# Branch A's output weights in three pieces, by 128, 104 and 24 partitions

## The chip, the core and the metric

The kernel runs on one core of one Trainium2 chip. The core has a matrix engine (TensorE, "PE" in the profile, its weight loads "PEld"), a vector engine (VectorE, "DVE"), a scalar engine (ScalarE, "ACT"), a general one (GpSimd, "POOL"), a sync engine that only issues transfers (SyncE, "SP"), 16 DMA engines that move data between the chip's memory (HBM) and the on-chip memory (SBUF, 128 partitions), and PSUM, where TensorE writes its sums. The metric is the device time of one execution in microseconds (us), lower is better. A time is compared with that of the kernel before, run on the same chip.

## What is computed

Two attention branches, A and B, each decode one token for two batch entries against a cache of 4096 tokens and 32 heads of 128 elements; a gate from the input mixes them:

```python
def _A_ref(x, k_cache, v_cache, wq, wo):          # x [2,1,512], caches [2,32,4096,128]
    q = (x @ wq).reshape(B, Sq, 32, 128).transpose(0, 2, 1, 3)
    scores = jnp.einsum("bhqd,bhkd->bhqk", q, k_cache) * (128 ** -0.5)
    p = _softmax(scores, axis=-1)
    o = jnp.einsum("bhqk,bhkd->bhqd", p, v_cache)
    return o.transpose(0, 2, 1, 3).reshape(B, Sq, 4096) @ wo   # wo [4096,512]
...
x = A_x
g = _sigmoid((x * gate_w).sum(-1, keepdims=True))
return g * a + (1 - g) * b                        # b: the same with B's caches and weights
```

Everything is float32. The caches are 4 x 134 MB, the four weight matrices 8.4 MB each: 570 MB have to be read once.

## The kernel before

**Tiles.** A unit is one batch entry and four heads of one branch: 16 units for A, 16 for B. A unit's K (and its V) is 16384 tokens of 128 elements, 128 rows of 64 KB, one row per partition. K goes into one of two 64 KB-per-partition tiles, `kt[0]` and `kt[1]`, in turn; V into the one tile `vt`. The weights use the K tiles too: the query weights `wq` of A and B come first, in `kt[0]` and `kt[1]`, and the output weights `wo` of A and B last, again in `kt[0]` and `kt[1]` (the table `place`, L206).

**Loops.** For each unit VectorE multiplies K by the query (L391) and sums over the 128 elements (L394), finds the maxima (L399 to L401) and makes the next query (L404, L405). ScalarE takes the exponentials (L365). TensorE multiplies these with V (L369), 32 chunks of four 32-row strips. A branch's 16 units run as loops on the engines, with semaphores between them that are written by hand.

**The order of the transfers.** All large loads are issued by SP, in one order written out in L516 to L526: `wq` A, first K, `wq` B, second K, first V, then K and V in turn; after the last K, `load_wo("A")`, the last V (in three pieces), and `load_wo("B")`. Before a K the wait is for its tile to be free (`k_free`, L231), before a V for `vt` (`v_free`, L239), before `wo` for the K tile (L245). The semaphore of a load counts 16 when all of it has landed.

**The output weights.** A matrix `wo` of 4096 by 512 lies as 32 rows of 512 elements (2 KB) in each of 128 partitions: partition p holds rows 32 p to 32 p + 31, which are 64 KB in one run in HBM. `load_wo` calls `load_parts`, which issues one load for each stretch of rows; for A a single stretch, 0 to OR = 32, on the semaphore slot "f"; for B six, with bounds 0, 16, 24, 28, 30, 31, 32 on six slots. `Streams.dma` (L97) issues a load and adds 16 to what the slot has to reach; it returns that semaphore and value, and `parts["wo", n]` keeps them.

**Who waits.** `arrived` (L213) makes an engine wait for pieces of a load. `project_out("A", OR)` (L575, body L489) waits once, before row 0, for entry 0 of `parts["wo", "A"]`; then it makes 32 products, one per row, into `most`. For B the products of rows 0 to 27 go into `most` too, with waits before rows 0, 16 and 24; ScalarE copies the sums out (L609), and the last rows (L512) and the fold of `most` (L612) are summed in another bank. Two copies (L621, L620) and two stores of the output end the kernel. Between A's product and that lie, on TensorE, branch B's `gather` (L473), the products with the last V (L369, `last_products`) and `deal_out("B")` (L482). POOL's L589 and what follows it reuse the tile of A's `wo`, and wait for A's product.

Of the kernel before, what the change touches and what calls it, by code (L numbers as in the profile page):

```python
# [12 lines left out]
P = 128  # L13
# [15 lines left out]
OR = H * DH // P  # L29
DQ = DH // OR  # L30
EARLY = OR - 4
# [110 lines left out]
def tile_gated_decode(ctx: ExitStack, tc: tile.TileContext, ins: dict, out: bass.AP):  # L142
# [12 lines left out]
    slot = small.tile([P, VC], F32, name="slot")  # L155
# [23 lines left out]
    with tc.tile_critical():  # L179
        S = Streams(nc, tc)  # L180
# [27 lines left out]
        parts = {}  # L208

        def load_parts(item, t, src, slots, *cuts):  # L210
            parts[item] = [S.dma("sp", t[:, i:j], src[:, i:j], slot=s) for s, i, j in zip(slots, cuts, cuts[1:])]
# [31 lines left out]
        def load_wo(n):  # L243
            i = place["wo", n]
            nc.sync.wait_ge(k_free[i], NU // 2)  # L245
            t = kt[i].rearrange("p r d -> p (r d)").rearrange("p (r e) -> p r e", e=D)
            for r in r_kt[i]:
                r.writers, r.readers = [], []
            load_parts(("wo", n), t, ins[n + "_wo"].rearrange("(p r) e -> p r e", p=P), *(
                ("f", 0, OR) if n == "A" else ("abchij", 0, OR // 2, 3 * OR // 4, EARLY, OR - 2, OR - 1, OR)))  # L250


        class Scratch:
# [8 lines left out]
        rows, ident, ones, xg, w, e = start(D), start(P), start(1), start(B * KC), start(P), start(1)  # L262
# [3 lines left out]
        def vput(e, make, reads=(), writes=(), **kw):  # L266
# [6 lines left out]
                                  slot="y"))  # L273
# [213 lines left out]
        wo = {}  # L487
# [33 lines left out]
        for u in range(2, NU):  # L521
            load_k(u)
            load_v(u - 1)
        load_wo("A")
        load_v(NU - 1)
        load_wo("B")  # L526

        spread_queries(0)
        for h in (0, 1):
            t = kt[0][:, h * NS // 2:(h + 1) * NS // 2]  # L530
            r = R()
# [84 lines left out]
        for i, e in enumerate(("dve", "act")):  # L616
            for j in range(STRIPS // OS):
                k = (i * STRIPS // OS + j) * QT
                src = acc[i][k:k + B, :D // STRIPS]
# [27 lines left out]
```

## Time and profile before

| | us |
|---|---|
| three runs, median | 1324.59 (1324.45 to 1324.62) |
| the profiled execution, its own time | 1324.58 |
| its span, first to last instruction | 1322.8 |

A row of the page or of a view names the line of the kernel, the engine, the operation, and "written tile <- read tiles". `x` is a count. In a timeline, the first number is the start in us from the start of the span, the second the time it took; a bracket at the end says how long the engine had stood idle before it and what it waited for. "SPq" is SP's own queue, where an issue of a transfer is an instruction. A "packet" is what one DMA engine moves at a time. q1 is the queue of the transfers that SP issues, q10 of those that ScalarE issues, and q8 and q14 fetch instructions. The "DMA share" is the mean busy share of the 16 engines: 1.0 says that all 16 are busy throughout; a short window can show a little more.

### The profile page before, as it was taken

Reading aid. Unit: us, or ns where it says so; the run is one execution under the profiler, and the core shown is the slowest. Engines: PE = TensorE matmul, PEld = TensorE weight load, DVE = VectorE, ACT = ScalarE, POOL = GpSimd, SP = SyncE. Lnnn points to the kernel's source line nnn. Section 1 sums busy time; section 2 is a strip of 40 time slices with the busy share of each in tenths; the row PEclk is TensorE's granted clock in tenths of the full one; section 3 lists DMA queues with packets and bytes.
Section 4 is the critical chain, followed back from the end, with each engine's and each line's share of the span. In section 5 each row is a group of like instructions: output and inputs, shape, how many; then the busy total and the mean of one; then the engine's idle time right before and its main releaser. Section 6 shows DMA issues by size and latency. Waiting matters only on the chain. (4 is left out here: it accounts for less than half of the span.)

```text
span 1322.8 us, 6257 instructions
## 1 busy us (share of the span) xinstructions
PE 343.3 (26%) x2406; PEld 100.7 (8%) x2406; DVE 1166.3 (88%) x321; ACT 101.4 (8%) x331; POOL 1.2 (0%) x8
## 2 busy tenths in 40 slices
PE   3202222202222221222224022222212222221256
PEld 0000000000000000000002000000000000000012
DVE  2399999999999999999999899999999999999960
ACT  0000000001010000101000010100001010000100
POOL 0000000000000000000000000000000000000000
PEclk9656666556666655666665566666566666656668
DMA  9999999999999999999999999999999999999998
GB/s 412 442 414 442 442 416 442 444 414 444 442 430 428 442 442 416 442 442 416 444 442 419 438 442 434 426 440 440 420 440 440 420 442 442 426 432 442 434 420 357
DMA packets 11109, 570.53 MB, mean 431 GB/s; under 512 B 1239, under 2 KB 1243, under 8 KB 1630
## 3 DMA queue, kind: packets, MB, share of 16 engines
q1 hardware_dynamic: 11092, 570.43, 99.6%
q8 instruction: 4, 0.07, 0.0%
q14 instruction: 3, 0.02, 0.0%
q10 hardware_dynamic: 10, 0.01, 0.0%
HBM read 570.43 MB, written 0.00 MB: 431 GB/s over the span
## 5 line engine op out<-in xcount | busy, mean ns | idle before, releaser
L391 DVE TENSOR_TENSOR kt<-kt,q 128x16384 f32<-128x16384 f32 x31 | 534.0, 17226 | 56.1 <-DVEq L95 56.0
L394 DVE TENSOR_REDUCE sc<-kt 128x128 f32<-128x16384 f32 x31 | 533.8, 17220 | 1.1
L369 PE MATMUL vp<-vt,pr 128*32 128x512 f32 x2048 | 291.8, 733 | 919.3 <-PEq L95 918.5
L369 PEld LDWEIGHTS vp<-vt,pr 128*32 128x32 f32 x2048 | 80.3, 132 | 1129.3 <-issue 1126.9
L365 ACT ACTIVATE pr<-sc,nm 32x128 f32<-32x128 f32 x128 | 50.9, 398 | 160.0 <-ACTq L95 118.2
L431 ACT ACTIVATE pr<-nil 128x512 f32<-128x512 f32 x31 | 19.3, 624 | 426.4 <-ACTq L95 426.4
L452 ACT ACTIVATE vs<-vp,slot 128x128 f32 (+1 forms) x16 | 5.9, 368 | 451.6 <-ACTq L95 451.6
L339 PE MATMUL qa<-kt,cols 128*2 128x512 f32 x128 | 18.7, 741 | 22.9 <-DMA kt<-in_B_wq_dram 15.7
L365 ACT ACTIVATION_READ_ACCUMULATOR pr<-sc,nm (+1 forms) x128 | 23.5, 184 | 0.0
L350 DVE STREAM_TRANSPOSE kt<-kt 128x1024 f32<-128x1024 f32 x1 | 1.2, 1246 | 23.5 <-ACT kt L348 23.5
L415 DVE SCALAR_TENSOR_TENSOR vs<-vp,slot,vs 128x128 f32 (+1 forms) x45 | 15.8, 351 | 6.3 <-DVEq L95 5.3
L534 DVE TENSOR_REDUCE sc<-kt 128x64 f32<-128x8192 f32 x2 | 17.4, 8686 | 0.1
L533 DVE TENSOR_TENSOR kt<-kt,q 128x8192 f32<-128x8192 f32 x2 | 17.4, 8686 | 0.0
L459 ACT ACTIVATE vp<-nil 128x512 f32<-128x512 f32 x15 | 9.0, 600 | 106.6 <-ACTq L95 106.6
L621 DVE COPY kt<-qa 2x128 f32<-2x128 f32 x2 | 0.6, 280 | 17.0 <-PE qa L512 17.0
L592 DVE TENSOR_REDUCE kt<-kt 128x32 f32<-128x128 f32 x1 | 0.4, 368 | 12.8 <-POOL kt L590 12.8
L497 PE MATMUL most<-kt,onA 128*2 128x512 f32 x64 | 8.6, 698 | 9.5 <-DMA kt<-in_A_wo_dram 9.5
L399 DVE TENSOR_REDUCE rm<-sc 128x1 f32<-128x128 f32 x31 | 8.7, 282 | 2.3
L405 DVE STREAM_TRANSPOSE q<-qsel 128x128 f32<-128x128 f32 x30 | 9.3, 311 | 1.3 <-DVE qsel L404 0.3
L602 DVE SCALAR_TENSOR_TENSOR vs<-vp,slot,vs 128x128 f32<-128x128 f32 x3 | 1.1, 352 | 10.6 <-DVEq L95 10.6
L350 DVE STREAM_TRANSPOSE vt<-vt 128x1024 f32<-128x1024 f32 x1 | 1.2, 1246 | 9.4 <-ACT vt L348 9.4
L497 PE MATMUL most<-kt,kt 128*2 128x512 f32 x56 | 8.6, 779 | 2.4 <-DMA kt<-in_B_wo_dram 2.4
(68 smaller groups left out, 72.9 us busy)
## 6 DMA issues: line engine op xcount, KB each, us to landing
kt<-in_A_wq_dram SPq DMA_DIRECT2D x2, 4096.0 KB, 16.6
kt<-in_A_k_cache_dram SPq DMA_DIRECT2D x2, 4096.0 KB, 29.0
vt<-in_B_v_cache_dram SPq DMA_DIRECT2D x1, 4096.0 KB, 18.3
kt<-in_B_wo_dram SPq DMA_DIRECT2D x1, 4096.0 KB, 33.1
vt<-in_B_v_cache_dram SPq DMA_DIRECT2D x1, 3072.0 KB, 25.2
kt<-in_B_wo_dram SPq DMA_DIRECT2D x1, 2048.0 KB, 37.5
vt<-in_B_v_cache_dram SPq DMA_DIRECT2D x1, 1024.0 KB, 27.2
kt<-in_B_wo_dram SPq DMA_DIRECT2D x1, 1024.0 KB, 39.5
```

The source lines that it names most:

```text
L339: put("pe", lambda x: x.matmul(t[h * QT:h * QT + B], cols[:, c], halves[:, c, i, h], start=c == 0, stop=c == KC - 1), [r_cols, *r_kt[i_k]] ...
L365: do(lambda x: x.activation(padded[h, :, b, j * VC:(j + 1) * VC], s[h].rearrange("p (c a) -> p c a", a=VC), AF.Exp, bias=m[h], accum_out=l ...
L369: return x.matmul(vp[c % STRIPS * QT:(c % STRIPS + 1) * QT], padded[:, c].rearrange("p b m -> p (b m)"), vt[:, c * VC:(c + 1) * VC].rearra ...
L391: at = D_.do(lambda x: x.tensor_tensor(kt[o], kt[o], q[:, None, :].to_broadcast([P, NS, DH]), op=ALU.mult), after)
L394: at = D_.do(lambda x: x.tensor_reduce(sc[o], kt[o], axis=AX.X, op=ALU.add), at)
L405: return D_.do(lambda x: x.transpose(q, qsel[:, 0].to_broadcast([P, DH // QT, QT])), at)
L415: at = D_.do(lambda x: x.scalar_tensor_tensor(vs[:, g], vp[:, a * DH:(a + 1) * DH], slot[:, a:a + 1], vs[:, g], op0=ALU.mult, op1=ALU.add) ...
L431: return A_.do(lambda x: x.activation(padded[:, :, b], nil[:, :, None].to_broadcast([P, NVC, G * VC]), AF.Copy))
L459: A_.do(lambda x: x.activation(vp, nil.to_broadcast([P, VC * DH]), AF.Copy))
L497: put("pe", lambda x: x.matmul(most[s * QT:s * QT + B], on[n][:, r], wo[n][:, r], start=n == "A" and r < STRIPS, stop=n == "B" and r >= EA ...
L533: put("dve", lambda x: x.tensor_tensor(t, t, q[:, None, :].to_broadcast([P, NS // 2, DH]), op=ALU.mult), [r_q], [r])
L534: put("dve", lambda x: x.tensor_reduce(sc[0][:, h * NS // 2:(h + 1) * NS // 2], t, axis=AX.X, op=ALU.add), [r], [R()])
```

## The change

Branch A's load of output weights, one stretch by 128 partitions before, is issued as three loads on the same slot "f": rows 0 to 29 by all 128 partitions (60 KB each), the last two rows by partitions 0 to 103 (4 KB each), and the last two rows by partitions 104 to 127 (4 KB each). The slot then counts to 48, and `parts["wo", "A"]` keeps the value of the last of the three, so that the one wait covers all. Branch B's load is as before.

```diff
@@ -246,8 +246,13 @@
             t = kt[i].rearrange("p r d -> p (r d)").rearrange("p (r e) -> p r e", e=D)
             for r in r_kt[i]:
                 r.writers, r.readers = [], []
-            load_parts(("wo", n), t, ins[n + "_wo"].rearrange("(p r) e -> p r e", p=P), *(
-                ("f", 0, OR) if n == "A" else ("abchij", 0, OR // 2, 3 * OR // 4, EARLY, OR - 2, OR - 1, OR)))
+            src = ins[n + "_wo"].rearrange("(p r) e -> p r e", p=P)
+            if n == "A":
+                for p, r in ((slice(0, P), slice(0, OR - 2)), (slice(0, 104), slice(OR - 2, OR)),
+                             (slice(104, P), slice(OR - 2, OR))):
+                    parts["wo", n] = [S.dma("sp", t[p, r], src[p, r], slot="f")]
+                return
+            load_parts(("wo", n), t, src, "abchij", 0, OR // 2, 3 * OR // 4, EARLY, OR - 2, OR - 1, OR)
```

## The prediction

> **What bounds the kernel now.** I read the page first: span, engines, transfers, queues.
>
> ```profile
> span 1322.8 us, 6257 instructions
> PE 343.3 (26%) x2406; PEld 100.7 (8%) x2406; DVE 1166.3 (88%) x321; ACT 101.4 (8%) x331; POOL 1.2 (0%) x8
> DMA  9999999999999999999999999999999999999998
> DMA packets 11109, 570.53 MB, mean 431 GB/s; under 512 B 1239, under 2 KB 1243, under 8 KB 1630
> q1 hardware_dynamic: 11092, 570.43, 99.6%
> q8 instruction: 4, 0.07, 0.0%
> q14 instruction: 3, 0.02, 0.0%
> q10 hardware_dynamic: 10, 0.01, 0.0%
> ```
>
> The 16 DMA engines are busy in every slice. VectorE, the busiest compute engine, leaves 12% of the span idle, so the kernel is a stream of 570 MB and its end is the end of that stream plus a short tail. Nearly all of it is one queue, q1, the one SP issues to.
>
> The counts also say how a load is spread. The issues, with KB where one size was recorded and the us to landing (A's K stands in two rows, the last V chunk's three pieces and B's six output weights in SP's timeline below):
>
> ```profile
> kt<-in_A_wq_dram SPq DMA_DIRECT2D x2, 4096.0 KB, 16.6
> kt<-in_A_k_cache_dram SPq DMA_DIRECT2D x2, 4096.0 KB, 29.0
> vt<-in_A_v_cache_dram SPq DMA_DIRECT2D x16, 28.3
> kt<-in_B_k_cache_dram SPq DMA_DIRECT2D x16, 42.6
> kt<-in_A_k_cache_dram SPq DMA_DIRECT2D x15, 42.6
> vt<-in_B_v_cache_dram SPq DMA_DIRECT2D x15, 28.4
> kt<-in_B_wq_dram SPq DMA_DIRECT2D x1, 40.2
> kt<-in_A_wo_dram SPq DMA_DIRECT2D x1, 42.6
> ```
>
> SP issues 77 loads by 128 partitions: query weights 3, K 33, V 34, branch A's output weights 1, B's 6. 77 x 128 packets, 77 x 16 completion packets and 2 + 2 for SP's half of the output are 9856 + 1232 + 4 = 11092: q1's row exactly. So a load of 128 rows is one packet per row, even for 64 KB rows, with a completion on each of 16 engines. q10 has 10: two rows of x with two completions, the one gate row with one, ACT's output half 2 + 2. The 1239 packets under 512 B are 1232 + 2 + 1 + 2 + 2. So 128 rows run on 16 engines, two on two, one on one.
>
> Next the chain of waits, in order of time, and SP's timeline.
>
> ```profile
> 1276.21 33.05 DMA kt<-in_B_wo_dram
> 1309.31 8.70 PE most L497 x56
> 1318.03 0.61 ACT kt L609
> 1318.68 0.40 PE qa L612 x8
> 1319.09 0.56 PE qa L512 x16
> ```
>
> ```profile
> 1237.61 0.33 SPq L104 DMA_DIRECT2D kt<-in_A_wo_dram  x1
> 1271.57 1.28 SPq L104 DMA_DIRECT2D vt<-in_B_v_cache_dram  x3
> 1276.21 4.70 SPq L104 DMA_DIRECT2D kt<-in_B_wo_dram  x6
> 1320.20 0.33 SPq L104 DMA_DIRECT2D out_dram<-kt  x1
> ```
>
> The last chain hangs on the arrival of branch B's output weights. Ahead of these in the same queue stand the last V chunk and, ahead of that, branch A's output weights, the load that is changed. Each engine takes its packets in order, so what an engine is given more at A's load it delivers later at B's.
>
> How level are the 16 engines? The windows view has, after the times, columns for PE, PEld, DVE, ACT and POOL busy, the clock, the mean DMA share and GB/s:
>
> ```profile
> 1237.00:1281.00 44.00, 10.47 (x68) 2.76 (x72) 37.70 (x14) 5.15 (x18) 0.00 (x0) 0.58 1.01 437
> 1281.00:1309.00 28.00, 20.72 (x160) 8.49 (x152) 2.05 (x8) 0.96 (x3) 0.50 (x2) 0.87 0.99 424
> 1312.00:1316.00 4.00, 4.00 (x35) 0.69 (x27) 0.00 (x0) 0.00 (x0) 0.00 (x0) 0.73 0.98 406
> 1316.00:1317.00 1.00, 1.00 (x16) 0.28 (x12) 0.00 (x0) 0.00 (x0) 0.00 (x0) 1.00 1.02 399
> 1317.60:1318.00 0.40, 0.39 (x9) 0.11 (x8) 0.00 (x0) 0.00 (x0) 0.00 (x0) 1.00 0.28 108
> 1318.00:1318.40 0.40, 0.40 (x16) 0.21 (x8) 0.00 (x0) 0.37 (x1) 0.00 (x0) 1.00 0.26 102
> ```
>
> and the same end cut into 40 slices of 0.05 us from 1317.5 us:
>
> ```profile
> GB/s 246 205 82 123 82 123 123 41 164 123 41 123 82 123 123 41 164 123 41 41 41 0 41 0 41 0 0 0 0 0 0 0 0 0 0 0 0 0 0 0
> ```
>
> Until 1317 us all 16 are full. From 1317.6 to 1318.4 us the share is 0.26 to 0.28, about 4 engines of 16: twelve are done, four run 0.8 us longer. In the slices the rate drops to single packets after the eighteenth, 1318.4 us, and the last is in the 25th, 1318.7 us: one engine is last by another 0.3 us. I read the four late ones as the engines that also fetched the four 16 KB instruction blocks of q8 (0.07 MB over 4), about 0.6 us of one engine's time each, but nothing in the views names an engine. The tail waits for that last one:
>
> ```profile
> 1280.23 8.61 PE L497 MATMUL most<-kt,onA 128*2 128x512 f32 x64 [9.51 <-DMA kt<-in_A_wo_dram]
> 1297.15 3.64 PE L369 MATMUL vp<-vt,pr 128*32 128x512 f32 x32 [0.81 <-DMA vt<-in_B_v_cache_dram]
> 1309.31 8.57 PE L497 MATMUL most<-kt,kt 128*2 128x512 f32 x56 [2.38 <-DMA kt<-in_B_wo_dram]
> 1316.58 0.10 PEld L497 LDWEIGHTS most<-kt,kt 128*2 128x2 f32 x4 [0.50 <-DMA kt<-in_B_wo_dram]
> 1317.89 0.33 PEld L512 LDWEIGHTS qa<-kt,kt 128*2 128x2 f32 x16 [0.94 <-DMA kt<-in_B_wo_dram]
> ```
>
> TensorE waits for B's pieces at 1309.31, 1316.58 and 1317.89 us, so a shift of the latest engine moves the end one for one.
>
> **The change, part by part.** Bytes: none added or removed; 128 rows of 64 KB before, 128 of 60 KB plus 128 of 4 KB after. One engine's rate is 437 / 16 = 27.3 GB/s (first window), so a 4 KB packet is 0.15 us and an engine's 32 KB share of the last two rows 1.20 us.
>
> *Two more issues on SP.* 0.33 us each by the row at 1237.61, up to 0.78 by B's six in 4.70 us. SP's next issue is at 1271.57 us, after a wait of 33 us for the V buffer. V's issue is not moved, so this costs 0; without that cover it would be 0.7 to 1.6 us of issue time, still ahead of a queue that lands A's load 42.6 us after its issue. Nothing else is queued behind on SP until then, and no wait is added.
>
> *Two more boundaries between loads in the queue.* The 28 us window holds the start of the three V pieces and of B's first at a share of 0.99: at most 0.28 us lost over four boundaries, 0.07 each. Two cost between 0 and 0.14 us; a gain has no source. I take 0, as the windows in which B's pieces follow each other stand at 0.98 and 1.02, on both sides of 1.
>
> *Smaller packets.* In 1316 to 1317 us, with 8 KB rows and below, a share of 1.02 moved 399 GB/s, 24.9 per engine. 32 KB at 24.9 in place of 27.3 GB/s is 1.32 against 1.20 us: between 0 and +0.12 us. I take +0.05, as the 4 KB rows lie in a mixed window.
>
> *How 104 and 24 rows spread.* This is the term that matters, and no row shows it. The counts above show equal whole shares, on 16, 2 and 1 engines for 128, 2 and 1 rows. Carried on, 104 rows run on 13 engines (8 each) and 24 on 12 (2 each). If both take the same engines, twelve get 40 KB in place of 32 (+0.30 us), one gets its 32 KB as before (0), and three get none (-1.20 us). No later load levels that out, as each gives all 16 the same. The end follows the latest engine:
> - it is one of the twelve: +0.3 us;
> - it is the one that stays as it was: 0, since the other three late ones, 0.3 us ahead, reach it at most;
> - it is one of the three unloaded: there are four late engines and only three places without load, so one late engine stays. If that has 32 KB as before, the end moves 0.3 us earlier; if 40 KB, it comes out at 0.
>
> So the term lies between -0.3 and +0.3 us, and I take 0, the middle, because no row names the late engines. [...]
>
> *Who waits for A's load.* Its wait now covers three pieces; TensorE's product with A's weights starts at 1280.23 us, after a 9.51 us wait. Queued behind on TensorE are branch B's gathers and V products, and POOL and VectorE prepare the end once A's product is done. If it comes 0.3 us later, TensorE next idles 0.81 us for V at 1297.15 us and 2.38 us for B's weights at 1309.31: 3.2 us of lateness by this route vanish. Cost 0.
>
> **Sum** against the profiled execution's own time, 1324.58 us (span 1322.8 and 1.8 around it; the median of the runs is 1324.59): 0 + 0 + 0.05 + 0 = 1324.6 us, with ends -0.3 and +0.3 + 0.14 + 0.12 = +0.6, so 1324.3 to 1325.2.
>
> **The rivals.**
> *Only powers of two.* If the spread goes by 16, 8, 4, 2, 1 (all counts seen fit that too), both pieces run on 8 engines: 13 and 3 rows, 64 KB in place of 32, +1.20 us: 1325.8 if the latest is among the eight, else about 0. For it: 128, 2 and 1 are powers of two. Against: nothing but that 13 divides 104 as well as 8 does.
>
> *Slower: the 104 rows fall on few engines.* In q10's row small counts run on few engines. If a count that 16 does not divide ran on one engine, it would carry 512 KB in place of 32, 480 x 1.024 KB at 27.3 GB/s, +18 us: 1342. It decides from four engines down (128 KB, +3.6 us, 1328.2). Against: two rows already use two, so it is no general fallback to one.
>
> *Slower: every load's fixed cost shows.* The output's store takes from its issue at 1320.20 to the end of the span, 2.6 us for a few KB. If the engines stood empty for that at each of two added boundaries, +5.2 us: 1329.8. Against: six pieces of B in one stream at a share of 0.98 to 1.02. [...]
>
> **How the numbers follow.** 0.2% is 2.65 us, about what a measurement of this kernel can tell from no change. Forecast (the three cases, 1324.3 to 1325.2): 0.88. Powers of two: 0.06, also within 0.2%. Few engines: 0.02. Fixed cost: 0.02. Faster by over 0.2%: 0.02, for something I have not seen, as levelling all engines perfectly could gain no more than about 1 us. So same 0.94, slower 0.04, faster 0.02. The range is 1324.0 to 1325.9: the forecast's ends, a little lower for run-to-run spread, and up to the powers of two.
>
> **What would show it.** Packets: 13 + 12 completions more and 128 data packets more give 11109 + 25 + 128 = 11262, with 1264 under 512 B; powers of two give 1255, 16 and 16 give 1271. The DMA share stays near 1.0 between 1237 and 1317 us. The tail shows its outlines: three engines done 1.2 us earlier, twelve 0.3 later. The waits of 9.5 us for A's weights and 2.4 us for B's first piece move by at most 0.3 us. I am wrong if the share dips after 1260 us, where the pieces run, or if the wait for B's first piece grows by microseconds.

## The result and the profile after

| | us |
|---|---|
| before, median of 20 runs | 1324.62 (1324.24 to 1325.42) |
| changed, median of 20 runs | 1326.64 (1326.23 to 1327.07) |
| ratio | 1.0015, 95% interval 1.0009 to 1.0022 |
| profiled execution of the changed kernel, its time and span | 1326.24 and 1324.4 |

The changed kernel is 2.0 us slower: under the 0.2% named in the prediction, yet no two of the 40 runs overlap, and it lies above the range. The profiled execution is one of the shortest; its span grew by 1.6 us.

The page after, its span, packets and two of its rows of transfers (KB, us to landing):

```profile
span 1324.4 us, 6259 instructions
DMA packets 11262, 570.53 MB, mean 431 GB/s; under 512 B 1264, under 2 KB 1268, under 8 KB 1783
q1 hardware_dynamic: 11245, 570.43, 99.6%
kt<-in_A_wo_dram SPq DMA_DIRECT2D x1, 7680.0 KB
kt<-in_B_wo_dram SPq DMA_DIRECT2D x1, 4096.0 KB, 34.9
```

The packet counts are those foretold: 11262, of which 1264 under 512 B, 25 more than before, as with 104 rows on 13 engines and 24 on 12. Branch B's first piece lands 34.9 us after its issue in place of 33.1, and its issue is where it was. So the time was lost in the queue ahead of it, as the chain of waits and SP's timeline after say too:

```profile
1277.37 42.12 DMA kt<-in_B_wo_dram
1319.49 0.04 issue
1319.53 0.62 PE qa L517 x16
```

```profile
1237.44 1.19 SPq L104 DMA_DIRECT2D kt<-in_A_wo_dram  x3
1271.39 1.60 SPq L104 DMA_DIRECT2D vt<-in_B_v_cache_dram  x3
1276.05 5.12 SPq L104 DMA_DIRECT2D kt<-in_B_wo_dram  x6
```

The chain now hangs on a later one of B's pieces, issued at 1277.37 us. SP begins each of these groups of issues no later than before; its last issue for B ends 0.3 us later (1276.05 + 5.12 against 1276.21 + 4.70), 30 us ahead of the first piece's landing. TensorE's products, from its timeline after:

```profile
1281.49 9.59 PE L502 MATMUL most<-kt,onA 128*2 128x512 f32 x64 [10.95 <-DMA kt<-in_A_wo_dram]
1310.99 6.78 PE L502 MATMUL most<-kt,kt 128*2 128x512 f32 x48 [1.64 <-DMA kt<-in_B_wo_dram]
1318.31 1.04 PE L502 MATMUL most<-kt,kt 128*2 128x512 f32 x8 [0.53 <-DMA kt<-in_B_wo_dram]
1319.53 0.62 PE L517 MATMUL qa<-kt,kt 128*2 128x128 f32 x16 [0.18 <-DMA kt<-in_B_wo_dram]
```

A's weights start their product 1.26 us later (1281.49 against 1280.23), B's 1.68 us later (1310.99 against 1309.31), and that shift stays to the end.

Where the queue lost it is seen in one stretch, 1274 to 1283 us, in which A's last rows run and V begins. The last two columns are the mean DMA share and GB/s. Before, then after:

```profile
1274.00:1283.00 9.00, 2.77 (x16) 0.55 (x20) 2.81 (x4) 1.96 (x8) 0.00 (x0) 0.50 0.86 372
```

```profile
1274.00:1283.00 9.00, 1.51 (x8) 0.26 (x12) 2.65 (x4) 1.96 (x8) 0.00 (x0) 0.50 0.99 343
```

Neither column alone tells it, as a packet of 64 KB (2.42 us by the packet records) can fall in or out of so short a stretch. Their quotient does: what 16 busy engines move. Before it is 372 / 0.86 = 433 GB/s, after 343 / 0.99 = 346. A busy engine moves less. The busy time beyond what the same bytes take at 433 GB/s is 9 x (0.99 - 343/433) = 1.8 us. I call this figure the loss of the stretch; with two digits for the share it is good to about 0.1 us. Before it is 0, as 433 is its own quotient.

The packet records of the trace show it too. I summed the bytes under way in steps of half a microsecond, on a clock of the DMA queues with its zero at the gate row's packet (rounded down):

```
GB/s by steps of 0.5 us from 1269 us on that clock
before   435 434 433 434 433 431 427 428 429 432 434 432 433 433
after    432 425 416 397 287 269 243 220 227 248 261 320 420 430
```

For over 3.5 us all 16 engines together run at some 220 to 320 GB/s, near half their rate. The 128 packets of 4 KB took 0.246 us on average, up to 0.466, the first ones 0.159.

These records also say in which packets the time was lost. Undisturbed, a packet of 60 KB takes 2.267 us, one of 4 KB 0.159, and one of V's first piece (32 KB) 1.213. What the packets took beyond that, summed and divided by 16 engines, is 0.11 us in the last packets of rows 0 to 29, 0.70 in the 4 KB packets and 0.90 in V's: 1.7 us together. So more than half of the loss lies in loads by 128 partitions, in packets that ran while other engines were still at the two pieces.

### The profile page after: what moved, and what is told of

It reads as the page before. It is cut to its first block, busy times and chain, and to the rows that moved or that the text cites. A ratio compares the mean times of both kernels' runs of the same rounds, so it can differ in the third digit from the quotient of the medians.

```text
span 1324.4 us, 6259 instructions
## 1 busy us (share of the span) xinstructions
PE 343.1 (26%) x2406; PEld 99.7 (8%) x2406; DVE 1166.3 (88%) x321; ACT 101.3 (8%) x331; POOL 1.2 (0%) x8
## 2 busy tenths in 40 slices
DMA packets 11262, 570.53 MB, mean 431 GB/s; under 512 B 1264, under 2 KB 1268, under 8 KB 1783
## 5 line engine op out<-in xcount | busy, mean ns | idle before, releaser
L478 PE MATMUL heads<-vs,pick 128*128 128x128 f32 x32 | 7.4, 415 | 11.9 <-DVE rs L475 10.0
## 6 DMA issues: line engine op xcount, KB each, us to landing
kt<-in_B_wo_dram SPq DMA_DIRECT2D x1, 4096.0 KB, 34.9
```

## The experiments

Two theories to start with. "Uneven shares": what the prediction summed, twelve engines with more bytes. "Shared paths", a conjecture that no row up to here shows: in a load by fewer than 128 partitions several engines write into the same group of partitions at once and halve each other's rate; the half is an estimate from the 220 to 320 GB/s above against 433. Against both stands that splitting as such costs. Times are medians beside runs of the kernel before on the same chip; the loss is worked out as above from the row that is shown.

**Two loads, both by 128 partitions.**

```diff
-                for p, r in ((slice(0, P), slice(0, OR - 2)), (slice(0, 104), slice(OR - 2, OR)),
-                             (slice(104, P), slice(OR - 2, OR))):
+                for p, r in ((slice(0, P), slice(0, OR - 2)), (slice(0, P), slice(OR - 2, OR))):
```

> Rows 0 to 29 of branch A's output weights by 128 partitions, the last two rows by 128 partitions too: one load more than before and the same 4 KB packets, with equal shares on all engines. Theory 'shared paths' (with a piece of fewer than 128 partitions several engines write into the same group of partitions at once and halve each other's rate): no loss, 1324.6 to 1324.8 us, and no stretch in which the DMA share stays near 1 while the rate falls. Rival 'splitting costs' (the boundary, or 4 KB packets with a 64 KB pitch): 1325.5 us or more, up to all of the 2.0 us.

1324.53 us against 1324.68, ratio 1.0000 (0.9991 to 1.0009).

```profile
1274.00:1283.00 9.00, 3.10 (x16) 0.55 (x20) 2.48 (x4) 1.96 (x8) 0.00 (x0) 0.50 0.98 420
```

429 GB/s, a loss of 0.1 us, and the 4 KB packets take 0.159 us at the median. One more boundary, 4 KB packets and their 64 KB pitch cost nothing that can be seen. What costs is the 104 and the 24.

**Two halves of 64 partitions.** Equal shares for all 16 engines.

```diff
-                for p, r in ((slice(0, P), slice(0, OR - 2)), (slice(0, 104), slice(OR - 2, OR)),
-                             (slice(104, P), slice(OR - 2, OR))):
+                for p, r in ((slice(0, P), slice(0, OR - 2)), (slice(0, 64), slice(OR - 2, OR)),
+                             (slice(64, P), slice(OR - 2, OR))):
```

> The last two rows by partitions 0 to 63 and by 64 to 127: both pieces on 16 engines, 4 rows each, so every engine carries its 32 KB as before. 'Shared paths': 8 packets of 4 KB at about 0.30 in place of 0.15 us on every engine, +1.2 us, 1325.8 to 1326.2 us. Rival 'uneven shares' (the loss comes from twelve engines that carry 40 KB): equal shares, 1324.6 to 1324.8 us.

1327.14 us against 1324.68, ratio 1.0017 (1.0008 to 1.0026): +2.5 us, more than was expected and more than the change itself.

```profile
DMA packets 11269, 570.53 MB, mean 430 GB/s; under 512 B 1271, under 2 KB 1275, under 8 KB 1790
```

```profile
1274.00:1283.00 9.00, 0.27 (x4) 0.11 (x8) 2.77 (x4) 1.96 (x8) 0.00 (x0) 0.50 1.00 328
```

1271 is 1239 + 32, two loads more with 16 completions each: both halves run on 16 engines, and no engine has more bytes than another. Yet the loss is 9 x (1.00 - 328/433) = 2.2 us. Uneven shares are not needed for it. By the packet records, summed as above, 0.86 us of it lie in the 4 KB packets, under the 1.2 that was expected, and 1.04 in V's first packets, behind the 4 KB ones: 27 of the 32 KB packets took over 8% longer than their 1.213 us, the longest 2.36 us.

**Four rows in place of two.** The same three loads, twice the bytes by 104 and 24.

```diff
-                for p, r in ((slice(0, P), slice(0, OR - 2)), (slice(0, 104), slice(OR - 2, OR)),
-                             (slice(104, P), slice(OR - 2, OR))):
+                for p, r in ((slice(0, P), slice(0, OR - 4)), (slice(0, 104), slice(OR - 4, OR)),
+                             (slice(104, P), slice(OR - 4, OR))):
```

> The last four rows in place of two by 104 and 24 partitions: the same three loads with 8 KB packets. 'Shared paths': the loss goes with the bytes, twice the 2.0 us, 1328.0 to 1328.8 us. Rival 'a cost per load' (issue, boundary or completion): as the changed kernel, 1326.4 to 1326.9 us.

1328.66 us against 1324.68, ratio 1.0030 (1.0018 to 1.0042): +4.0 us, twice the change's 2.0.

```profile
1274.00:1283.00 9.00, 0.00 (x0) 0.00 (x0) 2.91 (x4) 1.96 (x8) 0.00 (x0) 0.50 0.90 218
```

The quotient is 242 GB/s, the loss 3.6 us. The cost goes with the bytes, not with the loads: the 8 KB packets took 0.61 us at the median, against 0.309 undisturbed. The time alone would fit uneven shares too, which also double; packets that take twice as long would not.

**The same cut 1.2 ms earlier,** in branch B's query weights.

```diff
+            if n == "B":
+                t = kt[place["wq", n]].rearrange("p r d -> p (r d)")
+                src = ins[n + "_wq"].rearrange("(p c) f -> p (c f)", c=KC)
+                for p, r in ((slice(0, P), slice(0, 15 * 1024)), (slice(0, 104), slice(15 * 1024, 16 * 1024)),
+                             (slice(104, P), slice(15 * 1024, 16 * 1024))):
+                    parts["wq", n] = [S.dma("sp", t[p, r], src[p, r], slot="c")]
+                return
```

> Branch A's output weights in one piece as before; the same cut (60 KB by 128, 4 KB by 104 and by 24) is made in branch B's query weights instead, 1.2 ms earlier. If what an engine loses in the queue stays to the end, as the prediction had it: +1.5 to 2.0 us, 1326.1 to 1326.7 us. Rival 'it levels out' (waits for free tiles absorb it, and only a place near the end costs): 1324.6 to 1325.0 us.

1326.00 us against 1324.68, ratio 1.0011 (1.0002 to 1.0020): +1.3 us. By the windows view, 40 to 50 us, before and in this kernel:

```profile
40.00:50.00 10.00, 7.92 (x48) 1.46 (x52) 0.00 (x0) 0.00 (x0) 0.00 (x0) 0.61 0.92 395
```

```profile
40.00:50.00 10.00, 6.03 (x40) 1.18 (x44) 0.00 (x0) 0.00 (x0) 0.00 (x0) 0.59 1.02 375
```

10 x (1.02 - 375/433) = 1.5 us lost there against 0.1 before, and 1.3 us arrive at the end after 1.27 ms. So a loss in the queue is kept: it did not level out. The time is 0.1 us under the expected stretch; by the rows, the loss itself was smaller here (1.5 us) than in the change (1.8).

**Where the packets are written.** Partitions 0 to 63 of the last two rows by eight loads of eight partitions: neighbours, or four apart.

```diff
-                for p, r in ((slice(0, P), slice(0, OR - 2)), (slice(0, 104), slice(OR - 2, OR)),
-                             (slice(104, P), slice(OR - 2, OR))):
-                    parts["wo", n] = [S.dma("sp", t[p, r], src[p, r], slot="f")]
+                last = slice(OR - 2, OR)
+                S.dma("sp", t[:, :OR - 2], src[:, :OR - 2], slot="f")
+                for j in range(8):
+                    S.dma("sp", t[8 * j:8 * j + 8, last], src[8 * j:8 * j + 8, last], slot="f")
+                parts["wo", n] = [S.dma("sp", t[64:, last], src[64:, last], slot="f")]
```

> Rows 0 to 29 by 128 partitions; of the last two rows, partitions 0 to 63 by eight loads of eight neighbouring partitions (0 to 7, 8 to 15, ...), then partitions 64 to 127 by one load. [...] 'Shared paths': four engines at a time on one group of four partitions, the packets about four times as long (0.6 us), eight of them +3 to 5 us on the eight engines that carry them, 1327 to 1330 us. Rival 'shares alone' (these eight engines carry 48 KB in place of 32, +0.6 us): at most 1325.3 us.

```diff
-                    S.dma("sp", t[8 * j:8 * j + 8, last], src[8 * j:8 * j + 8, last], slot="f")
+                    S.dma("sp", t[j % 4 + 32 * (j // 4):j % 4 + 32 * (j // 4) + 29:4, last], src[8 * j:8 * j + 8, last], slot="f")
```

> The same loads from the same rows in HBM as in f_same_set, on the same engines, but each of the eight writes eight partitions four apart (0, 4, ..., 28, then 1, 5, ..., and so on), so that its engines write different groups of four partitions; two of the 32 rows of a partition then hold another partition's weights, so the output is not the reference's. 'Shared paths': these packets run at full rate; what is left is the 64-partition load, about +0.6 us, and the uneven shares, up to +0.6 us: 1325.2 to 1325.9 us, at least 2 us below f_same_set. Rival (loads, bytes and shares decide, not where they are written): the same time as f_same_set within 0.3 us.

Neighbours (f_same_set) 1327.62 us, four apart (g_spread) 1327.31 us, before 1324.84: ratios 1.0022 (1.0013 to 1.0031) and 1.0019 (1.0010 to 1.0028). The first lies in its stretch, but its 4 KB packets took 0.283 us at the median, not the 0.6 that was expected; the second is 1.4 us above its own. A difference of 0.3 us, so by its number the rival won. But the pair was badly made: both kernels end with a load of 64 partitions, a kind that had just been shown to cost. The rows leave little between them, a loss of 2.4 and of 2.0 us. Neighbours, then four apart:

```profile
1274.00:1283.00 9.00, 0.19 (x4) 0.11 (x8) 2.83 (x4) 1.96 (x8) 0.00 (x0) 0.50 0.98 309
```

```profile
1274.00:1283.00 9.00, 0.64 (x4) 0.11 (x8) 2.87 (x4) 1.96 (x8) 0.00 (x0) 0.58 0.95 313
```

So the three kernels that follow leave the upper half's last two rows out. In the cut below, "..." stands for lines that all three share, and the notes behind "#" are added here.

```diff
+                    near = slice(8 * j, 8 * j + 8)
+                    apart = slice(j % 4 + 32 * (j // 4), j % 4 + 32 * (j // 4) + 29, 4)
+                    parts["wo", n] = [S.dma("sp", t[near, last], src[near, last], slot="f")]    # first kernel
...
+                    parts["wo", n] = [S.dma("sp", t[apart, last], src[near, last], slot="f")]   # second
...
+                    parts["wo", n] = [S.dma("sp", t[apart, last], src[apart, last], slot="f")]  # third
```

> As f_same_set without its 64-partition load, which had shared paths of its own in both kernels: rows 0 to 29 by 128 partitions, the last two rows of partitions 0 to 63 by eight loads of eight neighbouring partitions; the last two rows of partitions 64 to 127 are not loaded, so the output is not the reference's and the engines that would carry them have 32 KB less. The eight engines that carry the eight loads have the same 32 KB as before. 'Shared paths': 4 KB packets of about 0.3 us, +1.2 us and up to 1 us more while V starts: 1325.6 to 1326.8 us. Rival 'loads, bytes and shares decide': 1324.3 to 1324.9 us.

> The same loads from the same rows in HBM on the same engines as h_near (the upper 64 partitions' last two rows left out there too), each written to eight partitions four apart, so that two rows of a partition hold another's weights. 'Shared paths': full rate, no stretch with a low rate at a full DMA share: 1324.2 to 1324.9 us. Rival: as h_near within 0.3 us.

> As i_apart, but each load also reads the rows that belong to its partitions, 256 KB apart in HBM in place of 64 KB. If only the place of the writing counts: as i_apart, 1324.2 to 1324.9 us. Rival 'the pitch of the reads counts': as h_near, or slower.

| written to | read from | median | against 1324.71, ratio |
|---|---|---|---|
| neighbours | neighbours | 1325.76 | 1.0009 (1.0000 to 1.0018) |
| four apart | neighbours | 1324.95 | 1.0002 (0.9993 to 1.0011) |
| four apart | four apart | 1324.62 | 1.0000 (0.9991 to 1.0009) |

The intervals of the ratios overlap, but none of the first kernel's 11 runs (1325.33 us and up) is as short as the longest of the other two (1325.25 and 1325.24). The second is 0.05 us above its expected stretch, the others are inside. The rows, in the same order:

```profile
1274.00:1283.00 9.00, 2.00 (x12) 0.40 (x16) 2.76 (x4) 1.96 (x8) 0.00 (x0) 0.59 0.96 360
```

```profile
1274.00:1283.00 9.00, 2.77 (x16) 0.55 (x20) 3.16 (x4) 1.96 (x8) 0.00 (x0) 0.50 0.94 403
```

```profile
1274.00:1283.00 9.00, 3.07 (x16) 0.55 (x20) 3.01 (x4) 1.96 (x8) 0.00 (x0) 0.50 0.93 400
```

Written to neighbours, the quotient is 375 GB/s and the loss 1.2 us; four apart it is 429 and 430 GB/s, under 0.1 us. The packet records say the same: in the first kernel 46 of the 64 packets of 4 KB took longer than 0.17 us, up to 0.322; in the other two all 64 took 0.159 us. The first and second have the same loads, bytes and rows in HBM and, by their equal completions (64 for the eight loads in the first), as many engines; they differ in nothing but the partitions written. The third shows that reads 256 KB apart cost nothing either.

Two things stay open. g_spread differs from i_apart in its load of 64 partitions alone. So that one load of 0.25 MB lost 2.0 us, where 0.6 was expected; 1.1 us of it lie in V's first packets, and no run takes it apart further. And that the place of the writing decides is shown for the loads of eight partitions. For 104 and 24 it is an inference: the loads by 128 and the two halves rule out the boundary, the packet size and the shares as what is needed for such a loss, but no trace says which engine writes which partition.

## Why the prediction was wrong

**The bound, the place of the end and the cover held.** The stream of transfers decides: losses of 1.8, 2.2, 3.6, 1.2 and 0.1 us in the stretch came out as +2.0, +2.5, +4.0, +1.1 and about 0 us in the time (104 and 24, two halves, four rows, eight neighbours, two by 128). SP's two further issues (1.19 us in place of 0.33) cost nothing, and TensorE's start on A's weights, 1.26 us later, was taken up behind it: it still waits 1.64 us for B's.

**The spread held.** 13 and 12 engines, by the 25 completions; the powers of two, the single engine and the fixed cost per load are out. At the 2.6 us of the output's store for a boundary, the two loads by 128 would have cost 2.6 us more than one; they cost nothing (1324.53 us against 1324.68).

**The step that failed is "Smaller packets" (0 to +0.12 us, taken as +0.05),** and with it the rate on which this step and the one after it rest, 437 / 16 = 27.3 GB/s for one engine. Both take the rate of an engine in loads by 128 partitions and carry it over to loads by 104 and 24, as if the engines did not depend on each other. All large loads of before are by 128, so no row showed it; this cost should have been bounded from the other side, by a half of the rate or less. At half the rate 32 KB cost 1.2 us more per engine. Measured in its place: 4 KB packets of 0.246 us on average against 0.159, and a loss of 1.7 to 1.8 us, of which 0.70 lie in those packets and 0.90 in V's first ones behind them. So a half of the rate for the pieces alone would not have been the whole account either. That engines slow each other was not among the rivals. The change stayed under 0.2%, as forecast, only because the loss was small: the reasons given for it did not hold.

On shared paths the runs agree with the conjecture in direction: the 16 engines together fell to 220 GB/s, about half of 433, and eight loads of eight partitions four apart lost nothing (quotients of 429 and 430 GB/s, packets of 0.159 us). The size does not fit as well. The expectation for f_same_set has four engines at a time on one group of four partitions, and packets four times as long. No run shows such a group; measured were 0.283 us at the median there and at most 0.322 us with the eight neighbours alone (h_near), twice 0.159 and not four times. That each of the eight loads runs on 8 engines is shown by the completions of h_near: of 80 packets under 512 B between 1274 and 1283 us, 16 are of rows 0 to 29 and 64 of the eight loads. What the engines share, and which engine writes which partition, is in no trace.

**The signs.** The prediction called itself wrong if the share dipped after 1260 us or the wait for B's first piece grew by microseconds. Neither happened: the share was 0.99 in the stretch, and that wait went from 2.38 to 1.64 us. What moved beyond the 0.3 us allowed for was the wait for A's weights, from 9.51 to 10.95 us. A low rate at a full share was no sign on the list.

**Two readings of before.** The 28 us window does hold the starts of four loads, but not of V's first piece: A's product began at 1280.23 us, so A's load had landed and V begun before 1281. They are V's second and third pieces and B's first two; the term stays as it was. And the four instruction blocks of 16 KB took 0.89 to 0.96 us of an engine each by the packet records, not 0.6.

**The shares were nearly of the right size.** The prediction had +0.30 us for an engine with both pieces and -1.20 for one with none, 1.5 apart. The packet records can be followed engine by engine, since each engine's packets follow each other without a gap: over 1.18 ms of the stream 16 packets are under way for 97% of the time, before and after, and more than 16 for nearly all of the rest. Start of the seventh packet of V, on the clock of those records, for engines that had fetched no instructions:

```
before, eleven engines                 1278.89 to 1279.20 us
after, nine engines with both pieces   1280.76 to 1281.01 us
after, one engine with no piece        1279.58 us
```

The two groups after are 1.2 to 1.4 us apart. But both stand later than foretold, +1.8 us in place of +0.30 and +0.5 in place of -1.20: about 1.5 us are the same for all, even for an engine without a piece, which was held up in V's first packets. Two of the four late engines, those that had fetched their 16 KB early, were among the three without load, and the two that fetched later carry rows of the pieces and are now the last: this is the third case of the prediction, which by the shares alone comes out at 0. The last packet of the stream, a completion, starts at 1312.32 us on that clock before and 1313.97 after, 1.65 us later, and the span grew by 1.6: about the part that is the same for all. What uneven shares alone would do was not tried apart from this.

## What to carry to other kernels

When a kernel is bound by its transfers, cut a load along the free dimension and keep all 128 partitions: a second load by 128 cost nothing here (1324.53 us against 1324.68), while 0.5 MB by parts of them cost 1.3 to 2.5 us that no later load gave back. Judge such a stretch by GB/s divided by the DMA share: the slowed engines showed a share of 0.99 at a quotient of 346 GB/s, against 433 before. And a rate taken from rows of one shape of load was no rate for another shape (27.3 GB/s for an engine by 128 partitions, here down to 220 / 16 = 13.8); bound it from below before summing.

## What the runs showed of the hardware that was not expected

- The slowing reaches past the loads that cause it: V's packets, by 128 partitions, took up to 2.35 us in place of 1.213 after A's 104 and 24. On the engine that came first to V, which carried neither piece, the first one took 1.80 us.
- It starts late. Of the 4 KB packets that began in the first 0.7 us, all but two took 0.159 us; every later one took longer, at least 0.178. No run shows why.
- Two halves of 64 partitions, the evenest of the cuts, cost no less (+2.5 us, loss 2.2) than 104 and 24 (+2.0 us, loss 1.8); the intervals of the two ratios overlap.
- The 16 engines did not draw level again: before the change, an instruction block fetched at about 40 us on the queues' clock still had its engine more than 1 us behind the eleven above in V's last chunk, 1.24 ms on.
